# A convolution written to both partition halves by TensorE, and four smaller moves, in the start of a convolution-and-maxout kernel

## Chip, cores and metric

One core of a Trainium2 chip. The metric is the device time of one execution in microseconds (us), as a median of several executions.

## The reference

```python
# x: 8 x 4160 x 192; weight: 8 x 7; w1, w2, w3: 192 x 768; w_out: 768 x 192
w   = softmax(weight)                    # 7 taps for each of 8 heads of 24 channels
y   = causal_conv(x, w)                  # 7 taps along the sequence, per head
h   = maximum(maximum(y @ w1, y @ w2), y @ w3)
out = h @ w_out                          # 33280 x 192
```

## The kernel before

The 33280 tokens go through in 65 blocks of 512. TensorE does the convolution as matmuls with a band matrix (`band`). The maxout is rewritten as w3 y + max(max(w1 y - w3 y, w2 y - w3 y), 0). So the first layer needs only w1 - w3 and w2 - w3 (`wd`), which stand in the two halves of the 128 partitions, and w3 @ w_out (`m16`) is added in the second layer. As both halves of `wd` want the same 64 channels of y, `yd` holds each channel group twice, once in each half.

```python
def keep_warm(n, pool=psw, tag="w"):               # dummy matmuls
    ps = pool.tile([P, NBLK], FP32, tag=tag, name="idle")
    for _ in range(n):
        nc.tensor.matmul(ps[:], lhsT=idle[:, 0:P], rhs=idle[:], start=True, stop=True)

def make_wd(j0, j1):                               # w1 - w3 and w2 - w3
    f = slice(P * j0, P * j1)
    nc.vector.tensor_sub(out=wd[:, :, f], in0=ws[:, :, f], in1=w3s[:, :, f])

def conv_dense(t, copies, pools=((psw, "w"), (psw, "w"))):   # blocks 0 to 3
    yd = dense[t] = ydp.tile([P, NC, NBLK], FP16, ...)
    for n, slots_ in enumerate((range(4), range(4, 6))):     # 6 slots of 32 channels
        ps = pools[n][0].tile([P, NBLK], FP32, ...)
        for (q, b, row_lo, rlen, lo, hi, cc) in chunks_of[t]:
            for v in range(2):
                for g, s in enumerate(slots_):
                    h = (32 * s + 31 * v) // GRP
                    nc.tensor.matmul(ps[32 * g:32 * g + 32, lo:hi],
                                     lhsT=xz[t][v][0:rlen, q, 32 * s:32 * s + 32],
                                     rhs=band[0:rlen, h, cc:cc + hi - lo],
                                     start=(v == 0), stop=(v == 1), tile_position=(0, 32 * g))
        if n == 0:
            copies[0](out=yd[0:HALF, 0, :], in_=ps[0:HALF, :])
            copies[1](out=yd[HALF:P, 1, :], in_=ps[HALF:P, :])
        else:
            copies[2](out=yd[0:HALF, 2, :], in_=ps[0:HALF, :])

def cross(t, cs=range(NC)):                        # blocks 0 and 1: into the other half
    for c in cs:
        a, b = (slice(HALF, P), slice(0, HALF))[::-1 if c == 1 else 1]
        nc.vector.tensor_copy(out=yd[a, c, :], in_=yd[b, c, :])

def cross_dma(t):                                  # blocks 2 and 3: the same by DMA
    nc.sync.dma_start(out=yd[HALF:P, 0:NC:2, :], in_=yd[0:HALF, 0:NC:2, :])
    nc.sync.dma_start(out=yd[0:HALF, 1, :], in_=yd[HALF:P, 1, :])

def l1(t, j):                                      # one tile of the first layer
    for c in range(NC):
        for i in range(2):                         # lp and lq, one in each half
            row = slice(HALF * i, HALF * (i + 1))
            nc.tensor.matmul(ps[i][:, 0:N], lhsT=wd[row, c, P * j:P * (j + 1)],
                             rhs=y[row, c, 0:N], start=(c == 0), stop=(c == NC - 1))
    nc.scalar.activation(out=r[:, 0:N], in_=ps[0][:, 0:N], func=AF.Relu)
    nc.vector.tensor_max(out=hs[t][:, j, 0:N], in0=r[:, 0:N], in1=ps[1][:, 0:N])

# ... the order of the start, cut:
conv_dense(0, ...); keep_warm(4); ...; l1(0, 0); ...; l1(0, 1)
conv_dense(1, (nc.scalar.copy, nc.scalar.copy, nc.scalar.copy))
keep_warm(4)
cross(1)
make_wd(2, 3)
l1(1, 0)
# ... tiles of blocks 0 and 1, the last subtractions, transposes of w3, casts
conv_dense(2, (nc.scalar.copy, nc.vector.tensor_copy, nc.scalar.copy))
# ...
cross_dma(2)
make_m(0); make_m(1); l1(1, 4); st2(0, 0, NJ)      # st2: second layer
# ... then blocks 2 to 64: l1 of one block between st2 of the block before it
```

The softmax here doesn't subtract the row's maximum and nothing guards it: scores larger than these inputs give would overflow.

## Time and profile before

| | before |
|---|---|
| median of the 3 runs known before the prediction (lowest to highest) | 479.07 us (478.72 to 479.59) |
| span of the profiled run | 477.6 us |
| first layer of block 2 starts | 30.66 us |
| last VectorE maximum starts, then the tail | 470.53 us, 7.10 us |
| TensorE at full clock from | 10.37 us |

The kernel has three parts: a start of 30.66 us that is full of waits, a steady stretch in which TensorE is busy without a break (439.34 of 439.34 us in the prediction's stage line), and a tail. The stage lines and the timeline are read in the prediction. The chain of waits, followed back from the last instruction (start, length, what), goes through VectorE where block 1 begins:

```profile
14.30 0.69 DVE h L379
15.02 0.91 DVE yd L334
15.97 0.37 PE lq L374
```

The first of the three crossing copies of block 1 (`yd`, L334) takes 0.91 us on that chain, though the prediction's timeline has all three in 1.54 us.

### The profile page before, as it was taken

The page shows a single profiled execution, that of the slowest core. Times are in us where ns is not written, and L with a number is a line of the kernel's source. Part 1 is how long each engine was busy: PE and PEld are TensorE (multiplying, and loading weights), DVE is VectorE, ACT ScalarE, POOL GpSimd, SP SyncE. Part 2 cuts the span into 40 slices and gives each one's busy share as a digit, 9 for nine tenths or more (in the row PEclk, how much of TensorE's full clock was granted, in tenths as well). Part 3 has the DMA queues.
Part 4 walks back from the last instruction along what each step waited for, and adds up shares of the span by engine and source line. Part 5 has one row for each costly group of instructions (what it writes and reads, how often), then busy time and mean ns, then how long its engine had stood idle before and what let it go on. Part 6 is the DMA issues. An engine that isn't in the chain of part 4 may idle for free.

```text
span 477.6 us, 21859 instructions
## 1 busy us (share of the span) xinstructions
PE 470.7 (99%) x9042; PEld 392.3 (82%) x9042; DVE 365.7 (77%) x610; ACT 325.6 (68%) x610; POOL 213.2 (45%) x347
## 2 busy tenths in 40 slices
PE   8999999999999999999999999999999999999995
PEld 4478888888888888888788888888888888888995
DVE  4767778778777877877777787877778787777774
ACT  4757666676666767666676766667667666766664
POOL 3636543553454355255445534534553454455200
PEclk9999999999999999999999999999999999999999
DMA  8775866666765666657577667656676765764423
GB/s 191 166 198 151 238 186 175 179 180 162 197 192 159 175 172 185 169 162 201 152 193 183 181 164 205 177 152 190 171 183 166 201 180 153 190 172 107 107 76 100
DMA packets 68481, 81.68 MB, mean 171 GB/s; under 512 B 9342, under 2 KB 57470, under 8 KB 68382
## 3 DMA queue, kind: packets, MB, share of 16 engines
q1 hardware_dynamic: 55438, 49.51, 41.6%
q0 software_dynamic: 12928, 30.78, 21.2%
q8 instruction: 71, 1.16, 1.1%
q14 instruction: 28, 0.23, 0.2%
q10 hardware_dynamic: 16, 0.00, 0.0%
HBM read 30.31 MB, written 25.56 MB: 117 GB/s over the span
## 4 chain that ended last, share of the span: by engine, by line
PE 97%; DVE 1%; issue 0%; ACT 0%
PE lp L374 32%; PE po L418 30%; PE lq L374 26%; PE G L299 7%; PE idle L215 2%; PE D L318 1%; DVE h L379 0%; PE band_cols L237 0%; DVE yd L334 0%; DVE yd L325 0%; DVE w3s L258 0%; ACT yd L324 0%; DVE wd L254 0%; DVE m L284 0%; DVE o L428 0%
## 5 line engine op out<-in xcount | busy, mean ns | idle before, releaser
L379 DVE TENSOR_TENSOR h<-r,lq 128x512 f16<-128x512 f16 x390 | 267.2, 685 | 100.0 <-ACT r L378 98.6
L378 ACT ACTIVATE r<-lp 128x512 f16<-128x512 f32 x390 | 232.8, 597 | 138.6 <-PE lp L374 91.2
L374 PE MATMUL lp<-yd,wd 64*128 64x512 f16 x1170 | 315.6, 376 | 0.1
L374 PE MATMUL lq<-yd,wd 64*128 64x512 f16 x1170 | 314.7, 375 | 0.8 <-DVE h L379 0.6
L418 PE MATMUL po<-wo,h 64*128 64x192 f16 x3120 | 230.2, 243 | 0.0
L418 PEld LDWEIGHTS <-h 64*128 64x128 f16 x3120 | 186.2, 94 | 25.8
L374 PEld LDWEIGHTS <-wd 64*128 64x128 f16 x2340 | 163.9, 93 | 24.1 <-issue 4.2
L444 POOL DMA_DIRECT2D out_dram<-o x64 | 51.2, 799 | 237.0 <-DVE o L428 221.7
L357 POOL DMA_DIRECT2D yd<-ys x183 | 92.7, 512 | 1.8 <-ACT ys L344 1.0
L418 PE MATMUL po<-m,yd 64*128 64x192 f16 x780 | 86.9, 243 | 0.0
L428 DVE TENSOR_TENSOR o<-a,po 128x384 f32<-128x384 f32 (+1 forms) x132 | 71.4, 542 | 1.0 <-ACT a L427 1.0
L427 ACT COPY a<-po 128x384 f32<-128x384 f32 (+1 forms) x132 | 61.7, 468 | 1.8 <-PE po L418 1.8
L418 PEld LDWEIGHTS <-yd 64*128 64x128 f16 x780 | 54.7, 94 | 8.1
L151 POOL CAST x<-xf 112x960 f16<-112x960 f32 x60 | 59.6, 995 | 2.5 <-DMA xf<-in_x_dram 2.4
L344 DVE CAST ys<-G 128x512 f16<-128x512 f32 x61 | 39.2, 683 | 0.0
L299 PEld LDWEIGHTS <-x 112*32 112x32 f16 x2400 | 28.6, 96 | 12.7 <-issue 12.3
L344 ACT CAST ys<-G 128x512 f16<-128x512 f32 x61 | 32.9, 588 | 1.3
L299 PE MATMUL G<-band,x 112*32 112x103 f16 (+1 forms) x2400 | 33.3, 209 | 0.0
L215 PE MATMUL idle<-idle 128*128 128x512 f16 x24 | 9.2, 527 | 1.2 <-DVE idle L210 1.2
L170 POOL CAST xz<-xf 112x240 f16<-112x240 f32 (+2 forms) x15 | 4.9, 375 | 7.7 <-DMA xf<-in_x_dram 7.3
L215 PEld LDWEIGHTS <-idle 128*128 128x128 f16 x24 | 2.6, 122 | 5.5 <-issue 3.8
L318 PEld LDWEIGHTS <-xz 112*32 112x32 f16 x240 | 4.7, 107 | 2.5 <-DVE wd L254 0.8
(48 smaller groups left out, 47.2 us busy)
## 6 DMA issues: line engine op xcount, KB each, us to landing
xf<-in_x_dram SPq DMA_DIRECT2D x57, 420.0 KB, 4.5
out_dram<-o POOLq DMA_DIRECT2D x62, 384.0 KB, 4.2
yd<-yd SPq DMA_DIRECT2D x61, 192.0 KB, 3.7
yd<-ys SPq DMA_DIRECT2D x61, 48.0 KB, 3.8
yd<-ys POOLq DMA_DIRECT2D x61, 48.0 KB, 3.5
xf<-in_x_dram SPq DMA_DIRECT2D x8, 252.0 KB, 4.3
yd<-ys POOLq DMA_DIRECT2D x61, 32.0 KB, 3.5
yd<-ys SPq DMA_DIRECT2D x61, 32.0 KB, 3.4
```

The lines of the kernel that those rows point to most:

```text
L151: nc.gpsimd.tensor_copy(out=v[0:rl, q0:q1, :], in_=xf[0:rl, q0:q1, :])
L215: nc.tensor.matmul(ps[:], lhsT=idle[:, 0:P], rhs=idle[:], start=True, stop=True)
L299: nc.tensor.matmul(G[i][32 * g:32 * g + 32, lo:hi], lhsT=x16[0:rlen, cb:cb + 32], rhs=band[0:rlen, h, cc:cc + hi - lo], start=True, stop=T ...
L344: copy(out=slots[t][:, i, :], in_=convs[t][i][:])
L357: (nc.sync, nc.gpsimd)[n % 2].dma_start(out=yd[r0:r0 + rows, c, :], in_=slots[t][s0:s0 + rows, half, :])
L374: nc.tensor.matmul(ps[i][:, 0:N], lhsT=wd[row, c, P * j:P * (j + 1)], rhs=y[row, c, 0:N], start=(c == 0), stop=(c == NC - 1))
L378: nc.scalar.activation(out=r[:, 0:N], in_=ps[0][:, 0:N], func=AF.Relu)
L379: nc.vector.tensor_max(out=hs[t][:, j, 0:N], in0=r[:, 0:N], in1=ps[1][:, 0:N])
L418: nc.tensor.matmul(ps[b0, i][:, s % 2, :], lhsT=a, rhs=b, start=first, stop=last)
L427: nc.scalar.copy(out=a[:, ss, :], in_=ps[s0, 0][:, ss, :])
L428: nc.vector.tensor_add(out=outs[t][:, s0:s + 1, :], in0=a[:, ss, :], in1=ps[s0, 1][:, ss, :])
L444: qs[0].dma_start(out=bass.AP(tensor=out.tensor, offset=r * D, ap=[[D, n], [step * D, s1 - s0], [1, D]]), in_=ob[p0:p0 + n, s0:s1, :])
```

## The change

Its intent is to shorten the start. TensorE writes block 1's convolution to both halves itself, so three VectorE copies and four dummies go. The products w3 @ w_out are put between first-layer tiles, where TensorE has gaps. The last two subtractions go to GpSimd as one, three dummies before block 0 go, and the last store is issued on ScalarE instead of behind others on SyncE.

```diff
-    keep_warm(8, psp, "p")
+    keep_warm(5, psp, "p")
...
-        for n, slots_ in enumerate((range(4), range(4, 6))):
-            ps = pools[n][0].tile([P, NBLK], FP32, tag=pools[n][1], name=f"D{n}_{t}")
+        for n, slots_ in enumerate(((0, 1, 0, 1), (2, 3, 2, 3), (4, 5, 4, 5)) if twice else
+                                   (range(4), range(4, 6))):
+            ps = psw.tile([P, NBLK], FP32, tag="w", name=f"D{n}_{t}")
...
-            if n == 0:
+            if twice:
+                copies[n](out=yd[:, n, :], in_=ps[:])
+            elif n == 0:
...
-                    store(t, s - (s == 1), s + 1, (nc.sync,))
+                    store(t, s - (s == 1), s + 1, (nc.scalar if s == 3 else nc.sync,))
...
-    conv_dense(1, (nc.scalar.copy, nc.scalar.copy, nc.scalar.copy))
-    keep_warm(4)
-    cross(1)
+    conv_dense(1, (nc.scalar.copy, nc.vector.tensor_copy, nc.scalar.copy), twice=True)
...
     cast_w3(2)
+    transpose_w3(1)
+    make_wd(4, 6, nc.gpsimd)
     keep_warm(1)
     l1(0, 3)
-    make_wd(4, 5)
-    transpose_w3(1)
+    transpose_w3(2)
     l1(1, 2)
-    make_wd(5, 6)
     keep_warm(1)
     l1(1, 3)
-    transpose_w3(2)
+    keep_warm(1)
     l1(0, 4)
     nc.gpsimd.tensor_copy(out=wo[:], in_=wos[:])
+    make_m(0)
     l1(0, 5)
+    make_m(1)
     cast_dense(2, (nc.gpsimd.tensor_copy, nc.gpsimd.tensor_copy))
+    st2(0, 0, NJ)
+    l1(1, 4)
     conv_dense(2, (nc.scalar.copy, nc.vector.tensor_copy, nc.scalar.copy))
...
-    make_m(0)
-    make_m(1)
-    l1(1, 4)
-    st2(0, 0, NJ)
```

More of the change, by code (lines that the diff above doesn't have):

```diff
@@ L250, with make_wd @@
     m16 = const.tile([P, 2, D], FP16)
-    def make_wd(j0, j1):
+    def make_wd(j0, j1, eng=nc.vector):
         f = slice(P * j0, P * j1)
-        nc.vector.tensor_sub(out=wd[:, :, f], in0=ws[:, :, f], in1=w3s[:, :, f])
+        eng.tensor_sub(out=wd[:, :, f], in0=ws[:, :, f], in1=w3s[:, :, f])
     def copy_w3(copy, part):
@@ L306, in conv, with conv_dense @@
         xin.pop(t)
-    def conv_dense(t, copies, pools=((psw, "w"), (psw, "w"))):
+    def conv_dense(t, copies, twice=False):
         yd = dense[t] = ydp.tile([P, NC, NBLK], FP16, tag="yd", name=f"yd_{t}")
-        for n, slots_ in enumerate((range(4), range(4, 6))):
-            ps = pools[n][0].tile([P, NBLK], FP32, tag=pools[n][1], name=f"D{n}_{t}")
+        for n, slots_ in enumerate(((0, 1, 0, 1), (2, 3, 2, 3), (4, 5, 4, 5)) if twice else
+                                   (range(4), range(4, 6))):
+            ps = psw.tile([P, NBLK], FP32, tag="w", name=f"D{n}_{t}")
             for (q, b, row_lo, rlen, lo, hi, cc) in chunks_of[t]:
```

## The prediction

> **What bounds the kernel now.** I read the page's first and second part, then a table by stage, then the timeline of the first 31 us and of the last 5 us. TensorE is the bound:
>
> ```profile
> PE 470.7 (99%) x9042; PEld 392.3 (82%) x9042; DVE 365.7 (77%) x610; ACT 325.6 (68%) x610; POOL 213.2 (45%) x347
> ```
>
> By stage (length, then busy time and count of TensorE, weight loads, VectorE, ScalarE, GpSimd, then clock, DMA share, GB/s):
>
> ```profile
> 11.30:17.57 6.27, 6.06 (x96) 3.19 (x95) 4.67 (x10) 4.17 (x11) 3.87 (x7) 1.00 1.12 240
> 17.57:24.44 6.87, 6.25 (x56) 2.38 (x51) 5.77 (x10) 4.68 (x10) 5.11 (x13) 1.00 0.44 115
> ...
> 30.66:470.00 439.34, 439.34 (x8574) 374.24 (x8571) 344.15 (x566) 305.70 (x567) 199.90 (x307) 1.00 0.64 172
> ```
>
> From 30.66 us, where the first layer of block 2 starts, TensorE is busy without a break to 470 us. The change touches nothing in that stretch: compared engine by engine, the two programs stand in the same order from there on, but for the last store. So the change can only move the instant at which that stretch begins, and the tail after 470 us. Before 30.66 us the busy share is flattered, since it counts dummy matmuls (L215) and matmuls that overlap. What really happens is in the timeline around block 1 (start us, us, engine, line):
>
> ```profile
> 14.48 1.04 PE L215 MATMUL idle<-idle 128*128 128x512 f16 x4
> 15.45 0.39 PE L374 MATMUL lp<-yd,wd 64*128 64x512 f16 x1
> 15.97 0.37 PE L374 MATMUL lq<-yd,wd 64*128 64x512 f16 x1
> 16.30 0.37 PE L374 MATMUL lp<-yd,wd 64*128 64x512 f16 x1
> ```
> ```profile
> 15.02 1.54 DVE L334 COPY yd<-yd 64x512 f16<-64x512 f16 x3
> ```
>
> Dummies run from 14.48, and the first layer of block 1 then waits piece by piece for the three VectorE copies that put the convolution into the other partition half. Its last channel group starts at 16.51 us, where unhindered it would have been at about 15.88 (15.45 + 2 x 0.215).
>
> [...] the eight dummies from 4.97 us take 3.59 us, the four from 14.48 us 1.04 us; single records double in pace at 10.37 us. [...] 60 convolution matmuls at 24.44 us take 1.09 us, of which 0.2 is the last one, in 20 groups of four or of two: 0.045 us a group, whatever its width. [...]
>
> **The change part by part.** I walk the new order by hand with the durations of the trace.
>
> Dummies before block 0's convolution, 8 to 5: three at 0.427 us = 1.28 us less; it starts at 7.21 us, not 8.49. The band it needs is ready at 6.83, so nothing else holds it. It is on the path, but the clock is not released sooner: the convolution (1.84 us at half clock) ends at 9.05, and of the four dummies after it three now run at 0.427 us until 10.37 us. The first layer of block 0 starts at about 10.66 us, not 11.30: **0.64 us** gained, and about 0.1 more because its crossing copies are now done in time. Block 1's x, landed at 10.9 us, does not stop it. Block 1's convolution starts at 12.16, not 12.88.
>
> Block 1's convolution twice over: 30 groups, not 20, at 0.046 = +0.46 us. Out go four dummies (4 x 0.216 = 0.86) and three crossing copies (1.54 us of VectorE). In come three copies of 128 partitions from PSUM: two on ScalarE (0.59 us each, from the 128x512 copies at L344) and one on VectorE (0.68). The first group waits for ScalarE's casts to 12.52, the last starts at 13.81. The new holder is VectorE: it must first finish the copy of w3 and one maximum, so its copy runs 14.18 to 14.87, and the second channel group starts at 14.93, the third at 15.15 instead of 16.51: **1.36 us** gained so far.
>
> Subtractions 4 and 5 to GpSimd: [...] VectorE loses 2 x 0.56 us. GpSimd has room:
>
> ```profile
> 14.95 0.82 POOL L262 CAST w3h<-w3s 64x768 f16<-64x768 f32 x1
> 18.74 1.14 POOL L491 CAST wo<-wos 128x1152 f16<-128x1152 f32 x1 [2.97 <-DMA wos<-in_moe_w_out_dram]
> ```
>
> It sits idle for 2.97 us for w_out, and the weights of the subtraction landed by 15.7 us[...]. The reader of its result starts at 21.4.
>
> The weight products (18 matmuls, 0.6 + 0.6 us), spread between tiles of the first layer: same work, moved. They fill gaps left by VectorE, but take a PSUM buffer of the first layer's pool, so tile 5 of block 0 waits for tile 4's ScalarE pass: it starts at 22.92, the second product at 23.9, ten output matmuls at 24.5, tile 4 of block 1 at 24.98.
>
> Block 2's convolution then starts at **25.72 us, 1.28 later** than before (24.44). Behind it stand 50 output matmuls at 0.041 and one first-layer tile (0.65), so TensorE would reach block 2 at 29.58, 1.08 us earlier than now. But block 2 is still crossed by two DMAs:
>
> ```profile
> 26.23 0.64 SPq L338 DMA_DIRECT2D yd<-yd  x1
> 26.96 0.56 SPq L339 DMA_DIRECT2D yd<-yd  x1
> ```
> ```profile
> 30.68 0.38 PE L374 MATMUL lq<-yd,wd 64*128 64x512 f16 x1
> 31.02 0.37 PE L374 MATMUL lp<-yd,wd 64*128 64x512 f16 x1
> ```
>
> The first is issued 1.79 us after the convolution's start, the second 2.52. They land after 2.4 and 4.0 us (DMA view); the second, at 30.97, already holds the second channel group at 31.02. [...] The same pair for block 3 took 3.1 us. In the new order the second is issued at about 28.2 and lands at 30.5 to 31.3: the second channel group starts at 30.5 to 31.3, against 31.02. So most of the 1.1 us turns into a new wait; I keep **0.3 us** (-0.3 to +0.6).
>
> Last store on ScalarE's queue:
>
> ```profile
> 473.24 0.35 DVE L428 TENSOR_TENSOR o<-a,po 128x192 f32<-128x192 f32 x1 [0.17 <-ACT a L427]
> ```
> ```profile
> 474.54 0.45 SPq L444 DMA_DIRECT2D out_dram<-o  x1
> ```
>
> The data are ready at 473.59 us, the issue comes at 474.54, since SyncE spends 1.42 us on the store of the first two slices (an instruction fetch runs at 472.20) and 0.41 on the next. Issued from ScalarE at 473.65 it would land 0.9 us sooner, after the 1.75 us that it now takes. The previous store stays on SyncE: if that stalls as now it ends at 475.90, not 476.29, and the gain is 0.4. TensorE's program is 108 rows longer before this point, which moves the fetch some 2 us ahead of the stores; I expect **0.7 us**.
>
> Sum: 0.3 + 0.7 = 1.0 us; with a little for block 2 landing early, 479.07 - 1.15 = 477.9 us.
>
> **The rivals.** (a) The crossing DMA gives all back: for it speaks that the second channel group already waits on it and that its source comes 1.28 us later. With 4.0 us to landing the stretch starts 1.2 us late, and the time is about 479.5. Against it: the SyncE queue holds no x load at that instant. (b) The start pays in full: if the crossing lands in 2.2 us, the stretch starts 0.6 us early, with the tail 477.6; that the crossing takes no part, 477.1. (c) Fewer dummies let the clock fall back [...] Against it: outside the convolution's wait near 12.3 us and that at 14.1 to 14.9 us TensorE has work. (d) The subtraction or its shared access slows VectorE[...]
>
> **Range and chances.** 2% is 9.6 us. All that the change can reach is 30 us of start and 7 of tail, with about 2 us of waits to win and as much to lose. The runs before span 0.9 us by themselves. I give 476.9 to 479.1 us for 8 in 10, and within 2% at 0.98.
>
> **What would show it right or wrong.** The steady stretch keeps its length (439.3 us to the same instruction). Block 0's first layer at 10.6 to 10.7 us; third channel group of block 1 near 15.2; [...] block 2's convolution near 25.7; a wait of 0.5 to 1.5 us at block 2's first layer, ended by the crossing DMA; the last store issued on ScalarE within 0.1 us of VectorE's last addition. It is wrong if block 2 shows no such wait (then nearer 477), if the clock's release moves, or if the last landing is still SyncE's.

## The result

The changed kernel takes **482.21 us** (480.74 to 482.96, 4 runs) against 479.27 us (478.72 to 479.59, 4 runs) for the kernel before in the same rounds. The ratio is 1.0059, with a 95% interval of 1.0033 to 1.0085. Ratios here are the mean time of one kernel's fast runs over that of the other's of the same rounds, so they are not quite the ratio of the medians. The change makes the kernel 0.6% slower. It was predicted to take 477.9 us, with a range up to 479.1.

The profiled run of the changed kernel has a span of 481.2 us, 3.6 us more than before. Where the time comes from is read by comparing the same VectorE maximum in both traces:

| start of the maximum, us | before | after | difference |
|---|---|---|---|
| block 0, tile 0 | 12.86 | 11.03 | -1.84 |
| block 0, tile 1 | 14.30 | 12.76 | -1.54 |
| block 1, tile 0 | 17.55 | 18.30 | +0.75 |
| block 1, tile 3 | 22.97 | 24.91 | +1.94 |
| block 0, tile 5 | 24.98 | 27.67 | +2.69 |
| block 1, tile 4 | 28.36 | 29.70 | +1.35 |
| block 2, tile 0 | 32.27 | 34.83 | +2.56 |
| block 2, tile 3 | 37.06 | 41.40 | +4.34 |
| the last one | 470.53 | 475.08 | +4.54 |
| end of the span | 477.6 | 481.2 | +3.6 |

So the start begins well, loses 2.3 us between block 0 and block 1, loses again inside the stretch that was to stay unchanged, and wins 1.0 us in the tail. The first loss is seen in the chain of waits of the changed kernel:

```profile
11.34 1.34 PE D L320 x94
12.69 2.85 issue
15.54 0.70 PE D L320 x20
```

Block 1's convolution (`D`, now L320) stops in its middle, and what stands there is "issue": TensorE waited for nothing that the profile shows. The timeline has the same gap between the 98th and the 99th of the 120 matmuls, and behind it first-layer matmuls at half pace, two every 0.4 us where two every 0.21 us is usual (start, length, engine, line, idle time before):

```profile
11.27 1.42 PE L320 MATMUL D<-band,xz 112*32 112x103 f16 x98
15.54 0.70 PE L320 MATMUL D<-band,xz 112*32 112x103 f16 x22 [2.85 <-issue]
16.17 0.60 PE L378 MATMUL lp<-yd,wd 64*128 64x512 f16 x1
```

The table by stage (columns as in the prediction) shows the pace with the clock: the granted clock was half from inside the gap on (0.50 in the second line). The clock records give full from 4.49, half from 14.73 to 21.56 us, then full to the end.

```profile
12.00:15.54 3.54, 0.69 (x61) 0.54 (x46) 2.49 (x4) 0.64 (x2) 2.09 (x3) 0.89 1.11 234
15.54:19.54 4.00, 4.00 (x44) 2.02 (x45) 1.25 (x2) 1.78 (x4) 2.69 (x2) 0.50 1.08 230
```

A second gap of the same kind lies between block 2's third and fourth tile, at the second layer's L422:

```profile
39.74 0.40 PE L422 MATMUL po<-wo,h 64*128 64x192 f16 x5 [1.60 <-issue]
```

What does TensorE wait for, if nothing is shown? Its own instructions are a candidate. The DMA view of the stretch from 11 to 16.5 us names a queue that carries them, with one packet in that time (the last figure is the time of the queue's packets as a share of sixteen engines' time; over 100% means that packets overlap):

```profile
q1 hardware_dynamic: 1567, 1.29, 110.5%
q8 instruction: 1, 0.02, 1.5%
```

That one packet of 16 KB was served at 12.78 us (its start; it took 1.30 us), while the packets of q1, with the loads of x and weights, took 110.5% of the sixteen engines' time. I counted TensorE's instructions in the trace, two for each matmul (a weight load and the multiplication). The first gap lies just before number 447, the second just before 1215, which is 447 + 3 x 256. The whole trace has 18192 of these instructions (2 x 9096) and 71 packets of 16 KB on q8, which is 256 to a packet. So I take each packet for the fetch of one block of 256, and the gaps for boundaries between blocks.

The crossing of block 2, at the lines that the prediction showed at 30.68 and 31.02 us before:

```profile
32.72 0.38 PE L378 MATMUL lp<-yd,wd 64*128 64x512 f16 x1
33.22 0.37 PE L378 MATMUL lq<-yd,wd 64*128 64x512 f16 x1
33.58 0.37 PE L378 MATMUL lp<-yd,wd 64*128 64x512 f16 x1
```

The second channel group starts 0.86 us after the first, where 0.26 us is usual (see E9): a wait of 0.6 us. The subtraction on GpSimd, and VectorE's own subtraction just after it, beside GpSimd's cast of w_out:

```profile
16.38 1.80 POOL L254 TENSOR_TENSOR wd<-ws,w3s 128x768 f16<-128x768 f32 x1 [1.18 <-DMA ws<-in_moe_w_dram]
18.90 1.30 DVE L254 TENSOR_TENSOR wd<-ws,w3s 128x384 f16<-128x384 f32 x1
```

The tail: VectorE's last addition, then the store's issue on ScalarE's queue 0.04 us after the data are ready.

```profile
477.78 0.35 DVE L432 TENSOR_TENSOR o<-a,po 128x192 f32<-128x192 f32 x1 [0.17 <-ACT a L431]
478.17 0.38 ACTq L448 DMA_DIRECT2D out_dram<-o  x1
```

### The profile page after: what moved, and what is told of

It reads as the page before. It is cut to its first block, busy times and chain, and to the rows that moved or that the text cites.

```text
span 481.2 us, 21962 instructions
## 1 busy us (share of the span) xinstructions
PE 470.2 (98%) x9096; PEld 390.8 (81%) x9096; DVE 365.0 (76%) x606; ACT 325.0 (68%) x609; POOL 213.8 (44%) x348
## 4 chain that ended last, share of the span: by engine, by line
PE 95%; DMA 1%; ACT 1%; issue 1%; DVE 1%; SPq 0%; ACTq 0%
PE lp L378 32%; PE po L422 30%; PE lq L378 25%; PE G L299 7%; PE D L320 1%; DMA xf<-in_x_dram 1%; DMA yd<-yd 1%; ACT band L241 0%; PE idle L215 0%; ACT r L382 0%; ACT yd L328 0%; PE pt L269 0%; ACT xz L170 0%; DVE h L383 0%; PE pm L282 0%
## 5 line engine op out<-in xcount | busy, mean ns | idle before, releaser
L422 PE MATMUL po<-wo,h 64*128 64x192 f16 x3120 | 230.5, 243 | 1.6 <-issue 1.6
L422 PEld LDWEIGHTS <-h 64*128 64x128 f16 x3120 | 185.2, 94 | 28.8 <-issue 2.2
L422 PE MATMUL po<-m,yd 64*128 64x192 f16 x780 | 86.8, 243 | 0.0
L422 PEld LDWEIGHTS <-yd 64*128 64x128 f16 x780 | 54.7, 94 | 8.1
L320 PEld LDWEIGHTS <-xz 112*32 112x32 f16 x300 | 4.6, 98 | 5.7 <-issue 4.7
L320 PE MATMUL D<-band,xz 112*32 112x103 f16 (+1 forms) x300 | 5.4, 215 | 3.9 <-issue 2.9
L215 PE MATMUL idle<-idle 128*128 128x512 f16 x18 | 6.4, 478 | 1.2 <-DVE idle L210 1.2
```

The source lines that it names most:

```text
L320: nc.tensor.matmul(ps[32 * g:32 * g + 32, lo:hi], lhsT=xz[t][v][0:rlen, q, 32 * s:32 * s + 32], rhs=band[0:rlen, h, cc:cc + hi - lo], star ...
L422: nc.tensor.matmul(ps[b0, i][:, s % 2, :], lhsT=a, rhs=b, start=first, stop=last)
```

## The experiments

**Theory.** TensorE is held when its stream of instructions reaches a new block of 256 less than some 2.7 us after that block's fetch was served (the two gaps end 2.76 and 2.60 us after it). The change makes this happen: it puts 240 quick instructions (1.4 us) of block 1's convolution where the first boundary falls, and the stream is there at 12.48 us, when the fetch has not been served (12.78). That the loads made it late was not shown. The half clock follows from the hold (it begins at 14.73 us, in the gap that ends at 15.54). **Rivals.** The second convolution costs by itself, whatever the fetches do. Or the crossing DMA of block 2 gives everything back. Or the subtraction on GpSimd slows VectorE. Or fewer dummies let the clock fall.

| run | median, us (runs) | before in the same rounds | ratio, 95% interval | first fetch served, us | tail, us |
|---|---|---|---|---|---|
| E1 the change, block 1 as before | 479.18 (4) | 478.96 | 1.0008, 0.9992 to 1.0025 | 12.46 | 6.80 |
| E2 block 1 twice, alone | 481.71 (4) | 478.96 | 1.0054, 1.0039 to 1.0069 | 14.31 | 6.09 |
| E3 the change, 36 instructions more | 484.36 (1) | 478.96 | one look, state unknown | 11.33 | 6.11 |
| E4 the change, 192 more | 482.08 (4) | 478.96 | 1.0064, 1.0049 to 1.0079 | 5.41 | 6.12 |
| E5 the change, 84 more | 478.82 (4) | 479.21 | 0.9990, 0.9966 to 1.0015 | 7.91 | 6.11 |
| E6 E5, block 2's convolution early | 479.08 (6) | 479.21 | 0.9998, 0.9977 to 1.0019 | 7.52 | 6.11 |
| E7 the change, dummies in the convolution | 482.79 (4) | 479.21 | 1.0080, 1.0052 to 1.0108 | 12.36 | 6.12 |
| E8 the last store, alone | 478.73 (4) | 479.21 | 0.9991, 0.9967 to 1.0014 | 11.89 | 6.59 |
| E9 block 1 once, 84 more, convolution early | 477.66 (6) | 479.06 | 0.9980, 0.9965 to 0.9995 | 8.10 | 6.11 |
| E10 E6, subtractions on VectorE | 478.12 (6) | 479.06 | 0.9988, 0.9975 to 1.0002 | 7.02 | 6.12 |
| E11 the subtraction, alone | 479.65 (4) | 479.06 | 1.0016, 0.9993 to 1.0040 | 14.21 | 6.94 |
| E12 the kernel before, 108 more | 479.86 (4) | 479.06 | 1.0007, 0.9985 to 1.0030 | 7.30 | 6.09 |

E1 to E4, E5 to E8 and E9 to E12 ran on one chip each. All gave the right result. In the texts, "row" is one instruction of TensorE. This document names a boundary by the place of its hold: 447, 703, 1215.

### E1 and E2: take the twofold convolution out, and do it alone

E1 is the change with this put back:

```diff
-    conv_dense(1, (nc.scalar.copy, nc.vector.tensor_copy, nc.scalar.copy), twice=True)
+    conv_dense(1, (nc.scalar.copy, nc.scalar.copy, nc.scalar.copy))
+    keep_warm(4)
+    cross(1)
```

> The whole change but block 1's convolution, which is written once, with its four dummies and three crossing copies as before. Theory F (instruction fetch: TensorE runs dry at row 447 of its stream, where a new 16 KB block of instructions begins, because 240 rows pass in 1.4 us there): row 447 now lies in tile 3 of block 0's first layer, behind slow rows, so no hold over 0.5 us near 12.5 us and no half clock after it; time 478.0 to 479.5 us, so about 3 us under the changed kernel. Theory D (the fewer dummies ahead of block 0 and between the tiles let the clock fall): half clock again, 481 us or more. Theory W (the crossing DMA of block 2, which now comes later, costs the time): its wait stays, 480.5 us or more.

E2 is the kernel before with the opposite edit and nothing else.

> The kernel before with block 1's convolution written twice as the only change. F: row 447 falls on about the 95th of the 120 matmuls; a hold of 2.5 to 3.5 us there, half clock for 3.4 or 6.8 us after it, time 481 to 483 us. D: block 0's eight dummies are back, so the clock holds; at or under 479 us. W: the products and block 2's convolution stand where they stood, so no wait at block 2; at or under 479 us.

E1 takes as long as the kernel before (1.0008), with no hold and the clock full from 9.70 us on. E2 has nearly the whole loss (1.0054 against 1.0059). In its trace the convolution stops at the same number in the stream, for 1.70 us and not the 2.5 to 3.5 expected, and half clock follows from 17.06 to 20.48 us:

```profile
16.84 0.59 PE L320 MATMUL D<-band,xz 112*32 112x103 f16 x25 [1.49 <-issue]
```

So the loss belongs to block 1's twofold convolution, with the four dummies and three copies that went for it, and not to the three dummies before block 0, the products, the subtraction or the store. That the four dummies are not its cause is seen in E5, which lacks them too. E1 tells one thing more. It reaches block 2 at 30.03 us, 0.63 us earlier than before, yet its second channel group starts at 31.00 us against 31.02. The crossing DMA gives that gain back: the prediction's rival (a) is real, but here it is worth only what had been won.

### E3, E4 and E5: move the boundary, not the work

Three versions of the change cut the first dummies into narrower ones. They stream the same columns, but have more instructions, so every later boundary falls elsewhere in the work.

```diff
+    def keep_warm(n, pool=psw, tag="w", split=1, plain=0):
...
+        w = NBLK // split
+        for k in range(split * (n - plain) if split > 1 else 0):
+            c = k % split * w
+            nc.tensor.matmul(ps[0:32, c:c + w], lhsT=idle[:, 0:32], rhs=idle[:, c:c + w], ...)
...
-    keep_warm(6, psp, "p")
+    keep_warm(6, psp, "p", split=4)      # E3; 8 in E5; 16 in E4
```

In E4 two of the next five dummies are cut in four as well.

> The changed kernel with each of the first six dummies cut in four narrow ones: 18 matmuls, 36 rows more, in the same time. F: the hold stays at row 447 of the stream, so it comes 18 matmuls earlier in block 1's convolution, after about 80 instead of 98, and lasts 2.5 to 3.5 us. A wait for data (a PSUM buffer, a cast, the band) would stay at the 98th matmul. Time near 482 us under both, since only the place moves.

> The changed kernel with 96 narrow dummies more in the time of the old ones ahead of block 0: 192 rows. F: row 447 now is the third matmul of block 1's convolution, with slow rows (dummies, two first layer tiles) ahead of it, so the fetch is under way while TensorE still has rows: hold there under 1 us, no half clock after 12 us, and about 3 us gone: 478 to 480 us, unless a later block boundary is hit by a hold of its own. A wait for data: still a hold of 3 us at the 98th matmul, 482 us. [...]

> The changed kernel with each of the first six dummies cut in eight narrow ones (84 rows more, same time). Refined theory F: [...] releases TensorE 2.6 to 2.9 us after it is served. Then 84 rows move [...] its boundary to the 56th matmul of block 1's convolution, and the next boundary to tile 4 of block 0: holds of under 1 us at both, no half clock after 12 us; 478 to 479.5 us. If a fetch is asked for only at the boundary itself, the hold stays at 2 us or more, at the 56th matmul, with half clock after it: 481 us or more.

In E3 the gap moves 18 matmuls forward in the convolution and stays at the same number in the stream, so it is tied to the stream and not to the matmul. (It is 2.22 us long, under the 2.5 expected, and the single look's 484.36 us is 2 us over what I expected: its trace also has a wait of 2.31 us for block 2's crossing DMA, half clock after it, and a hold of 1.81 us at 388.8 us.) In E4 there is no gap at 447, as its fetch came at 5.41 us, but there is one at 703, in block 1's first layer. My expectation of a time near the kernel before was missed, in the way that it named as the danger:

```profile
18.36 0.37 PE L383 MATMUL lp<-yd,wd 64*128 64x512 f16 x1 [2.90 <-issue]
```

E5 is the same work with 84 instructions more. It has no hold, the clock stays full, and it takes 478.82 us, as long as the kernel before. That is the change without its loss: **the twofold convolution itself costs nothing that the runs can show**, where they would show a cost of some 0.7 us (the interval's upper end, 1.0015). E9 and E10 below say the same more directly: they differ in block 1's convolution alone and ran in the same rounds, and the mean with two of them is 0.55 us longer, with an interval of -0.25 to 1.35. So the predicted 0.46 us of work is neither shown nor excluded, and no gain from writing it twice is seen. E5 also starts block 2 early (29.89 us) and pays for it at the crossing:

```profile
30.72 0.37 PE L383 MATMUL lq<-yd,wd 64*128 64x512 f16 x1 [0.45 <-DMA yd<-yd]
31.38 0.37 PE L383 MATMUL lp<-yd,wd 64*128 64x512 f16 x1 [0.29 <-DMA yd<-yd]
```

The fourteen profiles show this of the hold. Among the first five boundaries of each, every one that was reached under 2.5 us after its fetch was served shows a hold (at most 2.00 us after it, E12 at 1215), no other does (E2 at 1215 was reached 2.89 us after it), and TensorE goes on 2.48 to 2.88 us after the fetch (times in us from the traces; a hold is counted from the start of the last matmul before the boundary, "stream there at", to the start of the next; the last three rows are some of those without):

| run, boundary | stream there at | fetch served | hold | fetch to going on |
|---|---|---|---|---|
| after, 447 | 12.48 | 12.78 | 3.06 | 2.76 |
| after, 1215 | 37.90 | 37.14 | 1.85 | 2.60 |
| E2, 447 | 15.14 | 14.31 | 1.70 | 2.53 |
| E3, 447 | 11.99 | 11.33 | 2.22 | 2.88 |
| E4, 703 | 15.09 | 15.64 | 3.27 | 2.72 |
| E6, 1215 | 32.16 | 31.20 | 1.52 | 2.48 |
| E12, 1215 | 36.19 | 34.19 | 0.57 | 2.57 |
| before, 447 | 19.80 | 14.77 | none | - |
| E2, 1215 | 37.26 | 34.37 | none | - |
| E9, 447 | 12.74 | 8.10 | none | - |

Two holds came late in the program as well: 1.26 us in E2 at 399.3 us and 1.81 us in E3 at 388.8 us, both ended 2.6 us after their fetch. The kernel before has none at 447 (the stream is there 5.03 us after the fetch): at 14.77 us it still had some 67 instructions of the slow first layer to work through. The first fetch was served at 5.4 to 8.1 us in all kernels with at least 84 instructions more among the first dummies, and at 11.3 to 14.8 us in all others. The trace does not show when a block is asked for, so why the fetch comes earlier with more instructions was not shown.

### E7: fill the hold with dummies

```diff
         for n, slots_ in enumerate(...):
+            if twice and n == 2:
+                keep_warm(14)
```

> The changed kernel with 14 full dummies (14 x 0.216 = 3.0 us) between the second and third sweep of block 1's convolution: they stand just ahead of row 447, so TensorE works while the fetch is on its way. F: the time to the end of that convolution stays as long as with the hold (about 3 us of dummies, hold under 0.7 us), but the clock does not fall: what it gains over the changed kernel is the clock's share of the loss, 1 to 2 us, so 480 to 481.3 us. If the half clock cost nothing: 482 us. If the hold had nothing to do with the queue running dry, both would add: 484 us or more.

This was to tell the hold from the half clock. The 14 dummies covered the hold, and the clock stayed full to 34.6 us. Block 1's tile 4 then comes 1.75 us earlier than in the changed kernel (27.95 against 29.70), and that is an estimate of what the half clock cost at the start there. But block 2's crossing now waited 0.49 and 1.89 us at 31 us, beside an instruction fetch at 30.98, and half clock followed at 34.6. The time is 482.79 us, and the expectation was missed. The share of the clock in the whole loss is not settled by this.

Over the fourteen profiles, from the start of one matmul to the start of the next, the five gaps of 1.89 us and more were each followed by half clock, within the gap or at most 1.3 us after it. Of three gaps from 1.70 to 1.85 us one was, and of those up to 1.52 us none. So the length of the gap alone does not tell which fell. In each trace the clock's changes lie whole multiples of 3.41 us apart. Cut each trace at that pace from its first change on, and leave out the windows from the last matmul's end on: of the others, the six in which TensorE, by its records, was idle longest (1.49 to 2.24 us) are the six that ended in a fall to half clock. The next had 1.48 us (E6) and no fall. The window in which the last matmul ends is among those left out: it had 1.72 us without TensorE in the kernel before (from 471.16 us) and 1.54 in the changed kernel (from 475.53), and the clock fell only at the end of the window after it, at 477.99 and 482.36 us. So the idle time in a window, as counted here, does not decide the fall by itself, and what does was not shown. The changed kernel's second gap, 1.85 us, was split by a window's end at 38.62 us, with 0.48 us idle in the one window and 1.12 in the other, and E3's 1.81 us likewise, and neither was followed by half clock.

### E8: the last store alone

```diff
-                    store(t, s - (s == 1), s + 1, (nc.sync,))
+                    store(t, s - (s == 1), s + 1, (nc.scalar if s == 3 else nc.sync,))
```

> The kernel before with only the last store moved to ScalarE. Prediction's step: 0.4 us less as long as SyncE stalls on the store of the first two slices at the same instant as now (a fetch at 472.2 us), so 478.6 us. Theory F for the tail: what made the tail 0.95 us shorter in the changed kernel is the place of the fetch (the experiment with the old last store and the longer stream had the short tail too, 6.1 us after the last maximum against 7.07), so the queue by itself brings 0 to 0.4 us: within noise of the kernel before.

478.73 us, a ratio of 0.9991 that includes 1. The tail is 6.59 us here, 6.11 in the changed kernel, and 6.09 in E2 and E12, where the last store is still on SyncE. What goes with the tail is the last instruction fetch. Where it was served 1.7 to 2.3 us after the last maximum (before, E1, E8, E11), one of SyncE's store issues took 1.0 to 1.4 us in place of 0.35 to 0.45 and the tail is 6.6 to 7.1 us. In the other ten profiles it was served earlier (at the latest 0.7 us after the last maximum, in E4), no issue is stretched and the tail is 6.1, whichever queue issues the last store. The prediction's 0.7 us was right as a size, and so was its remark that the longer program moves the fetch: it was served at 472.20 us before, 1.67 us after the last maximum, and at 473.69 in the changed kernel, 1.39 us ahead of it. E2 and E12 have the short tail with the last store on SyncE, so the move to ScalarE was not needed for it. Where an issue is stretched the move may help: the tail is 6.59 and 6.80 us with it (E8, E1), 6.94 and 7.10 without (E11, before).

### E11 and E10: the subtraction alone, and the subtraction taken back

E11 is the kernel before with this edit.

```diff
+    make_wd(4, 6, nc.gpsimd)             # after cast_w3(2)
...
-    make_wd(4, 5)
...
-    make_wd(5, 6)
```

> The kernel before with the subtractions of block 1's third channel group on GpSimd and nothing else. Theory: GpSimd's takes 1.8 us, VectorE's neighbour 1.1 to 2.3 us in place of 0.56, and as block 1 has slack at that place the time is the same, 478.5 to 479.7 us. Rival (it frees VectorE by 0.5 us and that reaches the end): 478.2 to 478.6 us with VectorE's neighbour still at 0.56 us.

GpSimd takes 1.80 us, as in the changed kernel. But in E11 the operands landed early, so it ran beside the crossing copies of block 1:

```profile
15.18 1.80 POOL L254 TENSOR_TENSOR wd<-ws,w3s 128x768 f16<-128x768 f32 x1
```
```profile
15.52 2.25 DVE L334 COPY yd<-yd 64x512 f16<-64x512 f16 x3
```

The three copies take 2.25 us, against 1.54 before and 0.93 in E9, where GpSimd held none of them up. Block 1's first maximum comes 1.21 us later than before; 0.50 us of that was there at block 0's second maximum, and 0.71 is the copies'. The time range held the median (479.65 us, runs from 478.28 to 481.20), but the reason given for it, slack at that place, was wrong in the profiled run.

The single records tell more. A crossing copy takes 0.287 us, the subtraction of 384 columns 0.558 and the copy of w3 0.687 when GpSimd is still. When one is lengthened by a GpSimd instruction beside it, it ends at a fixed distance from the end of that instruction, in all fourteen profiles: 0.143 to 0.148 us after it for the crossing copies, 0.405 to 0.418 for the subtraction, 0.544 to 0.548 for w3's copy. That is in each case its own duration less 0.14 us. By these ends VectorE's instruction did not run slower, it waited until GpSimd's was over. It goes the other way too. GpSimd's cast of w3 takes 0.82 us alone, and where it began during VectorE's subtraction it took 1.03 to 1.22 us and ended 0.68 us after the subtraction, again its own duration less 0.14 us. In these pairs the one that came second waited; in E6 (below) VectorE's subtraction, begun at 16.34 us, also waited for GpSimd's, recorded from 16.43. In E11 the first copy ran from 15.520 to 17.132 us (1.612 us, the worst wait) and GpSimd ended at 16.985. The 0.91 us copy on the chain of the kernel before is the same: GpSimd's cast of w3 ended at 15.772 us and the copy at 15.919. VectorE's maximum, which takes one operand from PSUM, kept its 0.69 us beside GpSimd (in the kernel before at 14.30 us, beside GpSimd's copy of w3 from 14.07 to 14.89). Why the two wait for each other was not shown.

E10 is E6 with the two subtractions back on VectorE.

> The run with 84 more rows and block 2's convolution early, with the two subtractions back on VectorE. Theory (two engines that read and write SBUF at once slow VectorE's subtraction): VectorE's subtraction, 2.31 us beside GpSimd's, is back at 0.55 to 0.60 us each, and the third channel group of block 1 is ready up to 0.7 us earlier. Time 477.5 to 479.0 us if the hold at row 1215 comes again, 477.0 to 478.0 if it does not. Rival (the subtraction on GpSimd costs VectorE nothing): VectorE's subtraction stays above 1 us.

In E6 VectorE's subtraction met two GpSimd instructions in a row, a cast (from 15.64 us, 0.82 long) and GpSimd's subtraction (from 16.43 us, 1.80 long), and it took 2.31 us. In E10 the same subtraction takes 0.55. First E6, then E10:

```profile
16.34 2.31 DVE L259 TENSOR_TENSOR wd<-ws,w3s 128x384 f16<-128x384 f32 x1
```
```profile
16.54 0.55 DVE L259 TENSOR_TENSOR wd<-ws,w3s 128x384 f16<-128x384 f32 x1
```

The median is 478.12 us. It is within the wider range that I gave and just above the narrower one for a run without the hold at 1215. There was no such hold, but a new wait for block 2's crossing DMA took its place:

```profile
30.28 0.39 PE L383 MATMUL lq<-yd,wd 64*128 64x512 f16 x1 [0.63 <-DMA yd<-yd]
```

### E12: the kernel before with 108 instructions more

The first six dummies are cut in eight, and four of the next eight in four.

> The kernel before with 108 more rows of narrow dummy matmuls (the same columns streamed in all, cut finer) and nothing else: it moves every later fetch of instructions and every block boundary in the streams, no work. Theory: the fetch that stalled SyncE's last store at 472.56 us falls elsewhere, tail 6.1 instead of 7.10 us; row 447 now falls in block 1's convolution as in the changed kernel, but its fetch comes early (before 10 us), so a hold there is under 0.5 us. Time 477.9 to 478.7 us. Rival (row 447 within the convolution of block 1 is enough for a hold, whenever it was fetched): a hold of 1.5 to 3 us at row 447 and 480 to 482 us.

The boundary at 447 now falls into block 1's convolution, as in the changed kernel, and there is no hold: its fetch came at 7.30 us, the stream at 13.87. So the place alone was not enough: with the fetch 6.57 us ahead of the stream there is no hold, with the fetch 0.30 us behind it (the changed kernel) there is, and the rival (480 to 482 us) falls. The tail is 6.09 us as expected. The time is 479.86 us and the expectation was missed, and the profiled run lost 0.93 us before block 1's first maximum, 0.37 of it by block 0's second. GpSimd's copy of w3 and its cast ran from 15.32 to 17.02 us, on two crossing copies that then took 0.905 and 0.848 us, which is the rest. The four runs are 477.25, 479.81, 479.91 and 480.05 us. Why one is 2.6 us faster cannot be told without its trace.

### E6 and E9: versions that might beat both

E6 is E5 with block 2's convolution put ahead of the products, so that the crossing DMA starts earlier.

```diff
     nc.gpsimd.tensor_copy(out=wo[:], in_=wos[:])
-    make_m(0)
-    l1(0, 5)
-    make_m(1)
     cast_dense(2, (nc.gpsimd.tensor_copy, nc.gpsimd.tensor_copy))
-    st2(0, 0, NJ)
-    l1(1, 4)
     conv_dense(2, (nc.scalar.copy, nc.vector.tensor_copy, nc.scalar.copy))
...
+    make_m(0); l1(0, 5); make_m(1); st2(0, 0, NJ); l1(1, 4)     # after cross_dma(2)
```

> The same with block 2's convolution moved ahead of the weight products, so that its crossing DMAs start some 3 us earlier. If the crossing is what holds block 2 once the fetch does not (block 2 starts at 31.0 us in the kernel with block 1 as before, although TensorE is there at 30.0), block 2's second channel group starts at 29.5 to 30.3 us and the time is 476.5 to 478.3 us, faster than both kernels. If the fetch still holds: 480 us or more.

The wait for the crossing DMA is gone, but the stream then met the boundary at 1215 at 32.16 us, 0.96 us after its fetch, and the VectorE subtraction took 2.31 us. The time is 479.08 us, and the expectation was missed:

```profile
33.68 0.25 PE L304 MATMUL G<-band,x 112*32 112x100 f16 x5 [1.31 <-issue]
```

E9 takes all of it together: block 1's convolution once, with `keep_warm(4)` and `cross(1)`, both subtractions on VectorE, block 2's convolution early, and 84 instructions more. It keeps the change's five dummies, the products after block 2's convolution, and the store on ScalarE.

> Block 1's convolution once (four dummies and three crossing copies, as in the kernel before), subtractions on VectorE, last store on ScalarE, but block 2's convolution ahead of the weight products and the first six dummies cut in eight (84 more rows of TensorE's stream). Theory (TensorE is held when its stream reaches a 256-row block whose instructions were fetched under 3 us ago): the first fetch is served near 8 us, so row 447 is reached without a hold; no hold over 0.3 us at rows 447, 703; crossing copies of block 2 land before its second channel group is wanted, which starts at 29.4 to 30.3 us (31.02 before); tail after the last maximum 6.1 us (7.10 before); clock full but for one window at most. Time 476.8 to 478.3 us, faster than both by 0.2 to 0.5%. Danger that the theory itself names: a hold at row 1215 of up to 1.8 us, as in the run with the early convolution and two of block 1, and then 478.3 to 479.3. Rival (the second convolution of block 1 costs its 0.46 us of work and no more, the rest is chance): the same as before, 478.7 to 479.3.

It takes **477.66 us**, 0.9980 of the kernel before (0.9965 to 0.9995), faster than both, and as expected. No boundary shows a hold, and block 2 starts at 29.05 us without a wait, its second channel group at 29.31 us where it was 31.02 before:

```profile
29.05 0.38 PE L383 MATMUL lp<-yd,wd 64*128 64x512 f16 x1
29.13 0.39 PE L383 MATMUL lq<-yd,wd 64*128 64x512 f16 x1
29.31 0.37 PE L383 MATMUL lp<-yd,wd 64*128 64x512 f16 x1
```

Its profiled run (span 475.2 us) is the fastest of the six, so the 2.4 us between the two spans overstates the gain, which is 1.0 us in the mean. A part of the early start in that run is that the clock was released at 3.92 us and not at 10.37, which came by chance (E8, with the same start as the kernel before, has 4.29). How much of the mean each of its parts gives was not measured.

## Why the prediction was wrong

**The step that failed** is the sizing of "Block 1's convolution twice over: 30 groups, not 20, at 0.046 = +0.46 us", and with it the step that no break comes after block 2's first layer. The work was sized about right: 98 of the 120 matmuls ran in 1.42 us without a break. What was missing is that those 240 instructions took TensorE to the next 256 at 12.48 us, before the fetch of these was served (12.78). The runs showed in its place a hold of 3.06 us, then a half clock (between block 1's first and fourth maximum, while it lasted, the difference grew by 1.2 us, from +0.75 to +1.94, and E7 gives 1.75 us as an estimate for all of it), and a second hold of 1.85 us that ended at 39.74 us. E5, with the same work and 84 more instructions ahead of it, has none of these and takes 478.82 us.

**Block 0 and block 1.** Block 0's first layer was predicted at 10.66 us and came at 9.20, as the clock was released at 4.49 us in this run, against 10.37 before. That was luck: E8, with the start of the kernel before, has 4.29. The third channel group of block 1 was predicted at 15.15 us and came at 17.00. Until the hold the walk was, if anything, too careful.

**The crossing DMA.** Right in kind and size: a wait of 0.6 us at block 2 (0.5 to 1.5 predicted), and E1, where the hold is absent, gives back its whole early start of 0.63 us. The convolution of block 2 came at 28.97 us and not at 25.72, because of the hold.

**The subtraction.** GpSimd's took 1.80 us and ended at 18.18 us, before w_out was there: GpSimd's cast of it came at 18.65, after a wait of 0.46 us for the load. Rival (d) named a cost on VectorE, and for the subtraction it fell there: VectorE's own took 1.30 us in place of 0.56 and ended 0.41 us after that cast. In the changed kernel this instruction is not on the chain of waits.

**The store.** Right in size: the tail fell by 0.99 us (0.7 predicted). Wrong in its cause, as E8, E2 and E12 show. The two times of rival (b) were summed with 0.9 us for the tail; with the 0.7 us that the prediction expects they are 477.8 and 477.3.

**Rival (c)**, a clock that falls back, came true (half from 14.73 to 21.56 us), but not by fewer dummies: E5 has just as few (E1 has four more) and keeps its clock. In the changed kernel it came in the hold.

**The steady stretch** did not keep its length, as the second hold lies in it. The order of instructions on each engine was the same, and that is what I had checked. That their numbers had all shifted by 108, and the boundaries with them, I used only for the tail, where it helped.

What stays open: the share of the half clock in the timed runs, which granted 0.996 on average and so, by my estimate, had half clock for about 3.8 us (0.004 x 480 x 2), or one window of 3.41; when a block's fetch is asked for, and the scatter of E12.

## What to carry to other kernels

Count the instructions of the busiest engine up to each stretch of many short ones, and see when the trace serves its instruction fetches: a boundary in such a stretch, with the fetch served at 12.78 us, cost a hold of 3.06 us here, where the work added was put at 0.46. A gap that the profile calls "issue" and that stays at the same place in the stream when work is moved was a fetch here (E3), and some more instructions earlier on removed it without removing work (84 did; 36 did not, and 192 brought the next boundary to a bad place). Before a step is given to GpSimd, look at which VectorE instructions will run beside it: here crossing copies, subtractions and the copy of w3 waited for GpSimd's to end (a copy took 1.612 us in place of 0.287), while the maximum kept its 0.69 us.
